# One core, attention with memory beside an MLP: two PSUM banks read crosswise, weight loads in streams of their own, and a new written-out order of all jobs

## The chip, the core and the metric

The kernel runs on one core of one Trainium2 chip. The metric is device time in microseconds (us) of one execution. Three runs of the kernel before gave 691.15, 692.08 and 692.50; the median is 692.08.

## The reference, cut to what matters

```python
x  = A_x                                  # 1 x 2048 x 512
xn = layernorm(x)
out = x + A(xn) + B(xn)

# A: 32 heads of 16, four segments of 512 positions
q, k, v = xn @ wq, xn @ wk, xn @ wv
for s in range(4):
    p     = softmax(q_s k_s^T * scale + causal mask)
    a_dot = p @ v_s
    a_mem = (phi(q_s) @ M) / (phi(q_s) @ z + 1e-6)      # the memory part; M = z = 0 for s = 0
    o_s   = g * a_mem + (1 - g) * a_dot                  # g = sigmoid(beta), one per head
    M, z  = M + phi(k_s)^T v_s, z + sum(phi(k_s))        # phi(t) = t + 1 for t > 0, else exp(t)
A = concat(o_s) @ wo

# B: MLP, 512 -> 1792 -> 512
B = gelu(layernorm(xn) @ w1 + b1) @ w2 + b2
```

All inputs and the output are fp32.

## The kernel before, in words

Products that need fp32 accuracy are made of three fp16 products (high x high, high x low, low x high), so weights and activations are split into a high and a low half first. The attention work is cut into 16 units: unit i is segment i // 4 and group i % 4 of eight heads. The MLP is cut into 16 pieces j: 256 positions and one half of the 1792 hidden columns.

The program is one long list of 1308 small jobs. `streams()` gives lists of jobs, each list in its own fixed order; the string `ORDER` names, letter by letter, from which list the next job is taken; `BANKS` says, digit by digit, which of the eight PSUM banks the next tile gets. Both were written ahead of time by a planner that is not part of the kernel. Each engine executes its own instructions in the order in which the jobs issue them, and waits at semaphores. A moved job thus moves on every engine and queue that it uses. The jobs that the texts below name:

- `("wl", m, k)` loads a part of a weight (SyncE's queue), `wm` sums its squares, `wf` makes a scale of the sum, `ws` splits a piece into halves. Parts are "qk", "QK", "RK" (the first, second, and last two groups of wq and wk), "v", "1a", "1b" (halves of w1), "2a", "2b", "o". `("par",)` loads beta and b1, `("par2",)` uses them. `X` loads and normalizes 256 positions, `Xt` transposes them, `ratio` makes a row of scales.
- `("T", i, 1)` and `("T", i, 0)` project keys and queries of unit i (twelve 512-column matmuls, L495), write the halves to DRAM (`kd`, `qd`) and read them back in another layout (`kst`, `qst`, L542).
- `M` finds row maxima of the scores: TensorE pairs on the upper and lower 64 rows (L636), VectorE reduces (L643). `R` sends the maxima through DRAM (`md`) into `qst`. `S` makes the scores again with the maximum taken off (L676), ScalarE takes exp (L681), GpSimd masks the diagonal (L690). `pv` and `PV` multiply with v (L705). `O` normalizes; its third part makes `oT` (L740, L741).
- `Z`, `Qd`, `Q`, `K`, `N`: the memory part. `Qd` is part 0 of `a_mem`: two products into two PSUM banks (L586), then ScalarE takes the denominator from one half of the partitions (L591) and VectorE the numerator from the other half (L592), for each bank. The tile `ame` has one buffer, and GpSimd still reads it for the unit before (L737).
- `D` is a column block of w1 (twelve 256-column matmuls), `G` gelu (another activation table is loaded for it, L778, and the first one again behind it, L896), `H` splits the result (GpSimd L785, ScalarE L786, GpSimd L787), `e` the product with w2 (six matmuls in pairs, L812), `out` the product with wo (L830), `A` loads the residual and adds b2, `warm` eight matmuls whose result nobody reads (L843).

Of the kernel before, what the change touches and what calls it, by code (L numbers as in the profile page):

```python
# [41 lines left out]
PARTS = ("qk", "QK", "v", "1a", "2a", "RK", "1b", "2b", "o")  # L42
LOADS = {"qk": 1, "QK": 1, "RK": 2, "v": 2, "1a": 2, "2a": 2, "1b": 3, "2b": 2, "o": 2}
# [12 lines left out]


def streams():
    keys, queries, nat, maxi, soft, vals_p, heads, memo, vals, norm, again, hid, act, mlp, outs, accs, wts = (
        [] for _ in range(17))  # L60
    for i in range(NU):
        s, g = divmod(i, NG)
        keys.append(("T", i, 1))
        queries.append(("T", i, 0))
        maxi += [("M", i, n) for n in range(12)] + [("R", i)]
        for h, ts in enumerate(((0, 2), (1, 3))):
            soft += [("S", i, t, n) for t in ts for n in range(3)]
            vals_p += [("pv", i, h, kb) for kb in range(3)] + [("PV", i, h)]
        heads += [("O", i, k) for k in range(3)]
        if s:  # L70
            memo += [("Z", i), ("Qd", i), ("Q", i)]
        if s < NSEG - 1:
            nat.append(("N", i))
            memo.append(("K", i))
        if g == 0:
            vals += [("V", s, b) for b in range(4)]
            outs += [("out", s, b) for b in range(4)]
    norm += [("X", 0, 0, 0), ("X", 0, 1, 0), ("X", 0, 0, 1), ("X", 0, 0, 2), ("X", 0, 1, 2)]
    for n in range(NSEG):
        for b in range(2):  # L80
            norm += [("X", n, b, k) for k in range(3)] * (n > 0) + [("Xt", n, b, k) for k in range(2)]
    again = [("ratio", n) for n in range(NSEG)]
    for j in range(NU):
        hf, fh = divmod(j, 2)
        hid += [("D", j, f) for f in range(FH)]
        act += [("G", j)] + [("H", j, c) for c in range(4)]
        if fh == 0:
            accs += [("A", 2 * hf + a, k) for a in range(2) for k in range(2)]
        mlp += [("e", j, n) for n in range(2 * FH)]
    for m in PARTS:  # L90
        if m != "RK":
            wts += [("wl", m, k) for k in range(LOADS[m])]
        if m == "qk":
            wts.append(("hold",))
        if m == "v":
            wts.append(("par",))
    split = [[("wm", m, k) for k in range(SQUARES[m])] + [("wf", m)] + [("ws", m, c) for c in range(len(SPLIT[m]))] +
             [("gate",)] * (m == "RK") for m in PARTS]
    zero = [("zero", 0), ("const",), ("zero", 1)]
    return [norm, again, wts, [("par2",)], zero, keys, queries, nat, maxi, soft, vals_p, heads, memo, vals, hid, act,  # L100
            mlp, outs, accs, [("warm", n) for n in range(14)], [("wl", "RK", k) for k in range(2)]] + split


ORDER = (
    "atacctcaetcttetcawvavcatwvcaxeacatxvdccwvxwfttyyyxbxyyuxgyyyzozoywouoxyccyzhoAzzAootAAppciiizAznpBiiABfBncAiBpi"
    "gzBszniipnzBiimchqqqiCBqBqiiioAoACBCCBCjjqiojqAjqjcioijoiCikskkBcmDskioBjiqiqCjjoijqCiqjsCqjDiftaoCCpgkkkpkjqCj"
    "oloojjljoloojiipkkkkiqihspqijqqipqijqiqjsjqqjaajfgpiiqkkkkmpliqqiooiqpDlqoDopohijjiojiijpolsjiqaqajqiqiqqiiqapk"
    "akmkktspaqijqiqjqiqajqbqajopijjgDfopkkkDkjjjlooooDlhjjjolqiqqiipkkkkjiqqijqqjjiqiqjjqiqiqiDkkkkmpliilfnplimpngr"
    "rmrjjponijqjqjinjipiskmkkmkaiijrijjoojiqsjqqjiqiiiqqkkkkihlqlfmlogojqjqjqqjjasoojmkkkkmqjiqjqjjaojjpipmooisikkk"
    "klpilhiofmgoooqiqpppqiqiqqqiiiqqpsosmoiqqiiqiqppsslooijqjojijojijoiaakkkkmpaijqjqjaqqqjiqqjiqjqiikmkkakbqiaqqah"  # L110
    "lolfqjjojqmjgjjoolmmkkkkmhjjoojjiitjiojiippkkkkliiilnfnimpligniinipmrrijjrsijqjqiqjiqjqiipkmkkksiqjqijqjqjiqjqi"
    "iqjqikmpkkkiprlqsphlfojmjgopjjlojpjoomokmkkkqiqisjojiqisjqiqijqqijqhiqqiiqjsqiiqppmkkkkilalofomqpgopaoooospmlaj"
    "qqqjqqjqjqiiqiqqqjqiqqipipooooiijooppoiaakkkkmajiqpisqqjiqjqjaiqaqhjqqqjqaaqmkkkkbjlfoljqjmjgojjqolmkkkkmmjjjoo"
    "jjioijoiiippkpkkkiinliifniiilnnimlgrpmjjrmjjjrrijikkpskkiqqijqiqijqqjiqjiqjqiqjiqiispqkpkskksqilqoplfojmjgjjjpo"
    "ooojolmkkkkiqjiqpsjiqiqijqjqiqijqjiqiqiqiiqqkksmkpikplolfjjqmjgjjjoooooklpkmkkjiiopjqiqijqjiqpjqiqijqiqqiqiiqik"
    "kpspkkqiplpoooopljjjqqqjqjjqooolkpskmkpkmqqqpqjpjqqqjqjqpqqjqjqqqkmkkkqlllqqqqqqqqqrrrr"
)

BANKS = (
    "050123614061756123401632157467410534702651305176254301741260523716405142730612547306651240651024615024612504612"
    "504650124650412650412650412650142650142650421607653420107642531076425031702531270531270531270132570132570132576"
    "135402761350427163054273106542736574326574326537425632754632574631072456310724563071245360712453620731620731067"
    "203617621073621073621073621037621037621037261702361475023671540263701524603175246031746013746013713460713471630"
    "471630463714067314056723410523674105236741052367410527410527410527410527410527140352671450326475103264751023674"
    "523674523647253647236547236475264735264107532410765324107265431067512043675120436751204736152047361520473615270"
    "346150312750317250317253107250371257013275027135027134650132754062751340621375460376054370567403056374065374065"
    "307645307645307642153076241076241076241076253410762534621075346210754316024310264310432610432610324610324612403"
    "246013752640163754207156437120564371205647312056473120564731206547321065473265104723607423460273460273642073642"  # L130
    "073642051736420157642031765420316750316705315631705630157630157630157306173504621357462017345620147536210436024"
    "136024316403216403216403216403216740536740536740536740536271406"
)


# [14 lines left out]
def infini_mixer_kernel(ctx: ExitStack, tc: tile.TileContext, x, wq, wk, wv, wo, beta, w1, b1, w2, b2, out):  # L150
# [15 lines left out]
    def dense():  # L166
        return dps.tile([P, 512], F32, name="ps" + next(bank), bufs=1)
# [385 lines left out]
    def log_recip(src, tmp):  # L553

        A.activation(tmp, src, AF.Ln)
        A.activation(tmp, tmp, AF.Exp, scale=-1.0)

    def newton(dst, src, tmp):

        V.tensor_tensor(src, src, tmp, op=OP.mult)  # L560
        V.scalar_tensor_tensor(dst, src, 2.0, tmp, op0=OP.subtract, op1=OP.mult)  # L561
# [18 lines left out]
    def a_mem(i, part):  # L580
        g = i % NG
        if part == 0:
            ps = dense(), dense()
            for b, p in enumerate(ps):
                r = slice(64 * b, 64 * b + 64)
                T.matmul(p, zrt[i][r], pqt[i, 0][r], start=True, stop=True)  # L586
            rd = rden[i] = sb.tile([P, 512], F32, name="rc")
            n = ame[i] = sb.tile([P, 512], F32, name="ame")
            for b, p in enumerate(ps):
                r, z = slice(64 * b, 64 * b + 64), slice(64 - 64 * b, 128 - 64 * b)  # L590
                A.activation(rd[r], p[z], AF.Copy, bias=1e-6, scale=qkcs[r, 0, g:g + 1])  # L591
                V.tensor_scalar(n[r], p[r], bg[r, g, 4:5], None, op0=OP.mult)  # L592
        else:
            rd = rden[i]
            t = sb.tile([P, 512], F32, name="rt")
            log_recip(rd, t)
            newton(rd, rd, t)
            G.tensor_tensor(ame[i], ame[i], rd, op=OP.mult)
# [275 lines left out]
    memo = {}  # L874

    def once(kind, n, make):
# [49 lines left out]
```

## Time and profile before

| | |
|---|---|
| profiled execution | 691.51 us, span 689.8 us |
| median of three runs | 692.08 us |
| TensorE busy | 681.8 us, 99% of the span |
| VectorE, ScalarE, GpSimd busy | 545.7, 502.9, 340.5 us |
| DMA traffic | 55.15 MB, 80 GB/s over the span |
| granted TensorE clock | 0.999 |

PE is TensorE, PEld its weight loads, DVE VectorE, ACT ScalarE, POOL GpSimd, SP SyncE, which only issues DMAs here. A matmul's end in this profile is modelled and matmuls overlap, so "busy" hides short waits; from the start of one matmul to the start of the next one sees more. In rows of a timeline and of the chain of waits the first number is the start and the second the length, in us.

### The profile page before, as it was taken

How to read it: one execution, taken by the hardware profiler on the slowest of the kernel's cores; microseconds unless marked ns; L12 is line 12 of the kernel's file. 1: busy time of each engine (PE TensorE's matmuls, PEld its weight loads, DVE VectorE, ACT ScalarE, POOL GpSimd, SP SyncE). 2: the span in 40 equal slices, each digit the busy share in tenths (PEclk: the TensorE clock that was granted, in tenths of full speed). 3: DMA queues.
4: the chain of work that ended last, by engine and by line, in shares of the span. 5: the costliest groups of instructions: out<-in, count | busy, mean ns of one | idle time of the engine just before them, and what ended most of it. 6: DMA issues, size and time to landing. Idle time of an engine off the chain costs nothing.

```text
span 689.8 us, 17163 instructions
## 1 busy us (share of the span) xinstructions
PE 681.8 (99%) x6465; PEld 399.8 (58%) x6465; DVE 545.7 (79%) x1740; ACT 502.9 (73%) x972; POOL 340.5 (49%) x526
## 2 busy tenths in 40 slices
PE   8999999999999999999999999999999999999997
PEld 7855655565654546566554557567564456656653
DVE  6999968897795887998797787888688696969442
ACT  4486897788786659856794796766795687878870
POOL 5355567456535334663435355454353545446752
PEclk9999999999999999999999999999999999999999
DMA  9856342421203322421213224231120415140101
GB/s 277 249 149 201 92 109 49 117 55 31 65 24 102 94 67 45 122 50 33 69 26 98 58 73 100 72 86 32 41 72 24 132 19 154 17 109 2 19 1 62
DMA packets 51792, 55.15 MB, mean 80 GB/s; under 512 B 4782, under 2 KB 40636, under 8 KB 51708
## 3 DMA queue, kind: packets, MB, share of 16 engines
q1 hardware_dynamic: 49404, 49.84, 24.9%
q0 software_dynamic: 2304, 4.20, 3.8%
q8 instruction: 51, 0.84, 0.5%
q14 instruction: 33, 0.27, 0.1%
HBM read 36.99 MB, written 17.04 MB: 78 GB/s over the span
## 4 chain that ended last, share of the span: by engine, by line
PE 85%; DVE 5%; ACT 5%; DMA 2%; POOL 1%; issue 1%; SPq 0%; POOLq 0%; DVEq 0%; ACTq 0%
PE ps L495 36%; PE ps L812 17%; PE ps L705 10%; PE ps L830 6%; PE ps L676 5%; PE ps L636 5%; DVE ps L643 3%; ACT pt L681 2%; PE ps L586 2%; PE ps L514 1%; PE ps L843 1%; PE ps L321 1%; DMA wks<-in_A_wk_dram 1%; DMA qd<-hl 1%; PE ps L617 1%
## 5 line engine op out<-in xcount | busy, mean ns | idle before, releaser
L643 DVE CUSTOM_DVE_ANT_0 ps<-ps,mask 128x512 f32<-128x512 f32 (+3 forms) x512 | 233.9, 523 | 14.1 <-PE ps L636 12.9
L681 ACT ACTIVATE pt<-ps,qkcs 128x512 f32<-128x512 f32 (+1 forms) x384 | 206.8, 624 | 37.3 <-PE ps L676 35.2
L812 PE MATMUL ps<-w2s,hT 64*128 64x512 f16 x1344 | 176.6, 375 | 0.1
L495 PE MATMUL ps<-xnT,w1s 128*128 128x256 f16 x1344 | 158.0, 273 | 0.0
L690 POOL TENSOR_SCALAR_AFFINE_SELECT pt<-pt 128x256 f32<-128x256 f32 x256 | 101.0, 421 | 98.2 <-ACT pt L681 97.2
L495 PEld LDWEIGHTS <-w1s 128*128 128x128 f16 x1344 | 127.2, 98 | 28.5 <-issue 11.6
L787 POOL TENSOR_TENSOR hT<-hh,hT 128x512 f16<-128x512 f32 x64 | 67.7, 1057 | 86.3 <-ACT hT L786 82.7
L812 PEld LDWEIGHTS <-hT 64*128 64x128 f16 x1344 | 76.3, 94 | 49.8 <-issue 5.9
L705 PE MATMUL ps<-pt,vt 128*32 128x512 f32 (+3 forms) x1024 | 77.1, 435 | 0.1
L771 DVE SCALAR_TENSOR_TENSOR hT<-ps,sc,sr 128x256 f32<-128x256 f32 x112 | 52.4, 478 | 26.9 <-PE ps L495 26.7
L643 DVE DVE_READ_ACCUMULATOR2_ANT mc<- 128x1 f32 x512 | 71.0, 139 | 0.0
L636 PE MATMUL ps<-kst,qst 48*128 48x256 f16 (+3 forms) x512 | 66.7, 297 | 1.1 <-DMA qst<-qd 0.3
L676 PE MATMUL ps<-qst,kst 50*128 50x512 f16 (+3 forms) x512 | 66.2, 297 | 0.0
L786 ACT ACTIVATE hT<-hh 128x512 f16<-128x512 f32 x64 | 36.6, 572 | 33.3 <-POOL hh L785 32.9
L705 PEld LDWEIGHTS ps<-pt,vt 128*32 128x32 f32 x1024 | 30.5, 109 | 43.0 <-issue 32.4
L785 POOL TENSOR_SCALAR hh<-hT,sc 128x512 f32<-128x512 f32 x64 | 42.2, 660 | 25.7 <-ACT hT L778 24.1
L735 POOL TENSOR_TENSOR nN<-nN,oT 128x512 f32<-128x512 f32 x16 | 20.3, 1269 | 61.1 <-DVE oT L561 61.1
L778 ACT ACTIVATE hT<-hT,b1t 128x256 f32<-128x256 f32 x112 | 46.5, 495 | 0.2
L495 PE MATMUL ps<-xnT,wqs 128*128 128x512 f16 x192 | 44.2, 380 | 0.0
L495 PE MATMUL ps<-xnT,wks 128*128 128x512 f16 x192 | 44.1, 379 | 0.0
L495 PE MATMUL ps<-wvs,xnT 128*128 128x512 f16 x192 | 44.0, 379 | 0.0
L830 PE MATMUL ps<-wos,oT 128*128 128x512 f16 x192 | 43.3, 379 | 0.6 <-POOL oT L741 0.6
(225 smaller groups left out, 883.1 us busy)
## 6 DMA issues: line engine op xcount, KB each, us to landing
kd<-hl SPq DMA_DIRECT2D x48, 128.0 KB
qd<-hl SPq DMA_DIRECT2D x48, 128.0 KB
kst<-kd SPq DMA_DIRECT2D x32, 192.0 KB
qst<-qd SPq DMA_DIRECT2D x32, 192.0 KB
acc<-in_A_x_dram SPq DMA_DIRECT2D x16, 256.0 KB
acc<-in_B_b_dram POOLq DMA_DIRECT2D x16, 256.0 KB, 4.2
out_dram<-acc SPq DMA_DIRECT2D x16, 256.0 KB
xt<-in_A_x_dram SPq DMA_DIRECT2D x14, 256.0 KB
```

The costliest lines, as they stand in the source:

```text
L495: T.matmul(p, wsl(ws, k, a), xsl(xs, k, b), start=s0 and i == 0, stop=s1 and i == 3 * n - 1)
L636: T.matmul(p[:, o:o + n], stk[i, 0][r, t, P * qb:P * qb + P], stk[i, 1][r, t, :n], start=True, stop=True)
L643: V.tensor_tensor_reduce(p[:, o:o + n], p[:, o:o + n], mask[:, 512 - n:], 1.0, -3e38, OP.add, OP.max, mc[:, 16 * b + 4 * t + qb:16 * b + 4 ...
L676: T.matmul(p[:, o:o + n], stk[i, 1][r, t, P * kb:P * kb + P], stk[i, 0][r, t, P * kb:], start=True, stop=True)
L681: A.activation(e[:, OFF[kbs[0]]:OFF[kbs[0]] + o], p[:, :o], AF.Exp, scale=qkcs[:, 1, i % NG:i % NG + 1])
L690: G.affine_select(v, v, pattern=[[0, 2], [1, P]], compare_op=OP.is_ge, fill=0.0, base=0, channel_multiplier=-1)
L705: T.matmul(p[32 * c:32 * c + 32, P * kb:], vt[s, kb][:, 4 * g + c, 16 * odd:16 * odd + 32], pt[i, 2 * c + odd][:, OFF[kb]:OFF[kb] + LEN[kb ...
L771: V.scalar_tensor_tensor(hz[:, fi, :], p[:, :256], col(F1 + fh), srow[hs][:, own], op0=OP.mult, op1=OP.mult)
L778: A.activation(z, z, AF.Gelu_apprx_tanh, bias=b1t[:, FH * (j % 2) + f:FH * (j % 2) + f + 1])
L787: G.tensor_tensor(hT[:, z, 1, :], t, hT[:, z, 0, :], op=OP.subtract)
L812: w = T.matmul(pes[j][a], hTs[fh][r, fi, u, P * a:P * a + P], w2s[r, fo, v, :], start=n == 0 and m == 0, stop=fi == FH - 1 and m == 2, ski ...
L830: T.matmul(p, o[:, u, P * b:P * b + P], wos[:, g, v, :], start=i == 0, stop=i == 3 * NG - 1)
```

## The change

Three edits. First, each weight part gets a stream of its own, so that its load can stand anywhere; before, all loads but those of "RK" were one stream, in which `hold` and `par` stood too. Second, `Qd` issues ScalarE's read of bank 0, VectorE's read of bank 1, ScalarE's of bank 1, VectorE's of bank 0; before, both engines read bank 0 and then bank 1. Third, `ORDER` and `BANKS` are written anew (1308 jobs and 1173 banks as before; a line of each is shown).

```diff
-    for m in PARTS:
-        if m != "RK":
-            wts += [("wl", m, k) for k in range(LOADS[m])]
-        if m == "qk":
-            wts.append(("hold",))
-        if m == "v":
-            wts.append(("par",))
+    wts = [[("wl", m, k) for k in range(LOADS[m])] for m in PARTS]
...
-    return [norm, again, wts, [("par2",)], zero, keys, queries, nat, maxi, soft, vals_p, heads, memo, vals, hid, act,
-            mlp, outs, accs, [("warm", n) for n in range(14)], [("wl", "RK", k) for k in range(2)]] + split
+    return [norm, again, [("hold",)], [("par",)], [("par2",)], zero, keys, queries, nat, maxi, soft, vals_p, heads, memo, vals, hid, act,
+            mlp, outs, accs, [("warm", n) for n in range(14)]] + wts + split
...
-    "atacctcaetcttetcawvavcatwvcaxeacatxvdccwvxwfttyyyxbxyyuxgyyyzozoywouoxyccyzhoAzzAootAAppciiizAznpBiiABfBncAiBpi"
+    "auauvfdcauufaExauuEaGxaGwEbyfaFFGyEaEGGuAzuFzegHHJHauFGJuGHiAHHhCHFIIBtHpHHppHIJppIpJpBjjqBJIIgjIqjtoKCIIoujqjK"
...
-    "050123614061756123401632157467410534702651305176254301741260523716405142730612547306651240651024615024612504612"
+    "012531714607252301476502431056712645213076407541623037541231607543273410265734012654012654061254065421065421056"
...
-            for b, p in enumerate(ps):
-                r, z = slice(64 * b, 64 * b + 64), slice(64 - 64 * b, 128 - 64 * b)
+            lo, hi = slice(0, 64), slice(64, 128)
+
+            def den(p, r, z):
                 A.activation(rd[r], p[z], AF.Copy, bias=1e-6, scale=qkcs[r, 0, g:g + 1])
+
+            def num(p, r):
                 V.tensor_scalar(n[r], p[r], bg[r, g, 4:5], None, op0=OP.mult)
+
+            den(ps[0], lo, hi)
+            num(ps[1], hi)
+            den(ps[1], hi, lo)
+            num(ps[0], lo)
```

Lines ahead of `a_mem` stand 6 lower in the new file and lines behind it 2 higher: L591 and L592 become L586 and L589, L542 becomes L536, L681 becomes L683.

Three places in the order of instructions follow; row names are those of the kernel, a number behind a name is the buffer.

SyncE, where unit 1's keys and queries go to DRAM and back, before:

```order
L534 DMA kd_94<-hl 8x16x512
L535 DMA kd_94<-hl 8x16x512
L536 DMA kd_94<-hl 8x16x512
L282 DMA w2s<-in_B_w_dram 128x5x512
L534 DMA qd_96<-hl 8x16x512
L535 DMA qd_96<-hl 8x16x512
L536 DMA qd_96<-hl 8x16x512
L542 DMA kst_92<-kd_94 48x4x512 x2
L542 DMA qst_90<-qd_96 48x4x512 x2
```

The same place now:

```order
L276 DMA w2s<-in_B_w_dram 128x5x512
L273 DMA w1s<-in_B_w_dram 128x5x128 x2
L793 DMA acc<-in_A_x_dram 128x512
L273 DMA w1s<-in_B_w_dram 128x5x128 x2
L266 DMA acc<-in_B_w_dram 128x4x128 x2
L528 DMA kd_94<-hl 8x16x512
L529 DMA kd_94<-hl 8x16x512
L530 DMA kd_94<-hl 8x16x512
L268 DMA oT<-in_B_w_dram 128x512 x2
L528 DMA qd_96<-hl 8x16x512
L529 DMA qd_96<-hl 8x16x512
L530 DMA qd_96<-hl 8x16x512
```

The 1280 KB load of w2 has moved from between the two sets of writes to ahead of both; two loads of 256 KB stand there now.

ScalarE around `Qd` of unit 11, with the semaphores that each row waits for, before:

```order
L681 ACTIVATE pt<-ps_7859,qkcs 128x256 [waits PE_49]
L681 ACTIVATE pt<-ps_7860,qkcs 128x256 [waits PE_49]
L591 ACTIVATE rc<-ps_7867,qkcs 64x512 [waits PE_49]
L591 ACTIVATE rc<-ps_7868,qkcs 64x512 [waits PE_49]
L681 ACTIVATE pt<-ps_7879,qkcs 128x512 [waits PE_49]
L681 ACTIVATE pt<-ps_7880,qkcs 128x512 [waits PE_49,Pool_49]
```

ScalarE there now:

```order
L683 ACTIVATE pt<-ps_7863,qkcs 128x512 [waits PE_49]
L683 ACTIVATE pt<-ps_7864,qkcs 128x512 [waits PE_49,Pool_49]
L586 ACTIVATE rc<-ps_7869,qkcs 64x512 [waits PE_49]
L586 ACTIVATE rc<-ps_7870,qkcs 64x512 [waits DVE_49]
L523 ACTIVATE hl<-ps_7879 128x512 [waits DMAHW3_49,DMAHW4_49,DMAHW2_49,PE_49]
L526 ACTIVATE phq<-ps_7879,qksc 128x512
```

The second read waits for VectorE now, and behind it stands the projection of the next unit in place of exps.

ScalarE near the end, from gelu of piece 14 to the first exps of unit 15, before:

```order
L778 ACTIVATE hT_115<-hT_115,b1t 128x256 x7
L786 ACTIVATE hT_115<-hh 128x2x256
L653 ACTIVATE mhl<-ps_9851 32x64
L653 ACTIVATE mhl<-ps_9852 32x64
L786 ACTIVATE hT_115<-hh 128x2x256
L896 ACT_TABLE_LOAD
L555 ACTIVATE nD<-oT 128x512
L556 ACTIVATE nD<-nD 128x512
L786 ACTIVATE hT_115<-hh 128x2x256
L786 ACTIVATE hT_115<-hh 128x256
```

The same place now:

```order
L780 ACTIVATE hT_115<-hT_115,b1t 128x256 x7
L788 ACTIVATE hT_115<-hh 128x2x256 x2
L655 ACTIVATE mhl<-ps_9849 32x64
L655 ACTIVATE mhl<-ps_9850 32x64
L788 ACTIVATE hT_115<-hh 128x2x256
L898 ACT_TABLE_LOAD
L549 ACTIVATE nD<-oT 128x512
L550 ACTIVATE nD<-nD 128x512
L788 ACTIVATE hT_115<-hh 128x256
```

Three copies of the split hidden layer stand ahead of the table load now, two did before.

More of the change, by code (lines that the diff above doesn't have):

```diff
@@ L58, in streams @@
 def streams():
-    keys, queries, nat, maxi, soft, vals_p, heads, memo, vals, norm, again, hid, act, mlp, outs, accs, wts = (
-        [] for _ in range(17))
+    keys, queries, nat, maxi, soft, vals_p, heads, memo, vals, norm, again, hid, act, mlp, outs, accs = (
+        [] for _ in range(16))
     for i in range(NU):
@@ L106 @@
[L106 to L115, printed above, removed]
@@ L116 @@
-    "kpspkkqiplpoooopljjjqqqjqjjqooolkpskmkpkmqqqpqjpjqqqjqjqpqqjqjqqqkmkkkqlllqqqqqqqqqrrrr"
+    "auauvfdcauufaExauuEaGxaGwEbyfaFFGyEaEGGuAzuFzegHHJHauFGJuGHiAHHhCHFIIBtHpHHppHIJppIpJpBjjqBJIIgjIqjtoKCIIoujqjK"
+    "jKKhKIJojqLqjoLjrjjrrrnJKLDrDjijKrjppKMLKJLtkJrkpkjrkjrjKJrkpkjpKjMLjllllpKkjtrjkpkjkrjLrLkLkgjnlLlLqltluhqppkL"
+    "krmppqmpkkkppkjrrjjmqlllljkrqrjkrkrjrkjrkrkarijgthpjrjqMrjjqrrnqlllljmappjjipqMkkmppkjkjpqkjrararjmkrjarjqjrtru"
+    "llanllktrjrarkjrkrbjraaMrkpnqpkjkhMqglalllkkmpqppkmikppkjrkrjjlllmlrjkrqjrkrjrkjrkjrkrrkjrjrMqjjllllMnjmmohmogs"
@@ new lines @@
+    "snkrkokkaopkjjskqjjllnllkqjjsnkktjppakjrrqkjrjrkrjjtlqlllirjmrmgpknhpkrkrkrkkptpllmlnlnkrjkrrkrkknpijkpjqjqjlll"
+    "lmtppmgpptqpnjqjhqrrrrjtrjjrqrjrqrjppjjrrjpjrjqmnrkrkppkkjpqjkpkjaajlqlllnrkjrakrkattrkrjnkrrirkrjjallllbarrjam"
+    "mpgpkrkrrkknkhpkmlnnlllkkpnpkipkjjkpukjjjqllllmojjmjgojmnjhojqjojqsqqsjkkskjrkrkrjrjrkjltlnllnkjrjrkjrknrkarkjr"
+    "rkjrjjqllttlqlsjmqripmgpkknhkkpprqkkpmpnllltlnjrkjrnrtiqkrjjrrjkpjrrjkrjrkjrrkjrjqjllllqmppmgjtnpqhppqppkrqrkra"
+    "rnkrrrkrjrjrtkrjrjrrjjmqppqppkjjajqpppjaalllqlnrjrqkarjrtkrirrakakjrrkrkrnraallllkrkmrmkgbknhpkkppllmnllnkkppnj"
@@ L117 @@
+    "kkpkjpjjklllqljqjojjqojmjqjjgmojnmhonskkksskkjsjkjllllnjkqrrjkrrjrkjrkjrkrktrjjrqjrttjlqlllrjmmrgprkknhppqpnkkk"
+    "npppmkjjlqllljjrkrjqrkjtrrkjrkjrkrrkjjrjrtqjllllrtjqmpmgrrkknqhpkkqppkkpmplnlltljjkqkjpkjrkjrkrjrkjrjrqjrjrqrjr"
+    "jrlllqljpqpmppqkmkrrrkkrkkrppptlmllnqqlnqrrrkqkrrkrrrrrkqkkrrrnrrllllrrrmrrrrrmmrrrssss"
 )
 BANKS = (
-    "050123614061756123401632157467410534702651305176254301741260523716405142730612547306651240651024615024612504612"
-    "504650124650412650412650412650142650142650421607653420107642531076425031702531270531270531270132570132570132576"
@@ L124 @@
[L124 to L132, printed above, removed]
+    "012531714607252301476502431056712645213076407541623037541231607543273410265734012654012654061254065421065421056"
@@ new lines @@
+    "421056421065421062514062514062514602514602514605021467324350167243507243502743052374035720437520437250431027456"
+    "310217405634217056340627315406257406274502674056270456247065247063752140623751406123754061237540612307361207361"
+    "207360127360127360127360172306176023637014015246732645017342635017345026170435261703461736041763064317430671604"
+    "173604173160471036471502367415023617450132467501234675034675034673504673540765431027654310276530412765310472652"
+    "047652047265047265407265405726405627405316247250134376520153476206145267301715604236175046234517063204517632307"
@@ new lines @@
+    "465123014723401721034721340712341072034172034102734610523712460572314560751476051047651047651045706145670145671"
+    "045623134705612035467501230451230453142503167436250174367204516324705163706513706513706513760513761075240137426"
+    "572301465672301425067531240675134206751304267513460274351620741634250702136457123604572134572413572413572413575"
+    "234123754615345021634765042137625047136125736125736151723651273635753126570431267504321673504216735246103752465"
+    "102546102645102645012641025641203561724601747216047246107246152"
```

## The prediction

> **What bounds the kernel now.** I read the page first, then TensorE's waits, then the chain of waits in order of time.
>
> ```profile
> span 689.8 us, 17163 instructions
> PE 681.8 (99%) x6465; PEld 399.8 (58%) x6465; DVE 545.7 (79%) x1740; ACT 502.9 (73%) x972; POOL 340.5 (49%) x526
> PE   8999999999999999999999999999999999999997
> PEclk9999999999999999999999999999999999999999
> ```
>
> TensorE is never idle for long in any slice and has its full clock; no other engine reaches 80%. The change neither adds nor drops an instruction (the counts of jobs are equal), so what it can alter is the time that TensorE spends between matmuls. For that I need the pace within a kind of work. Four rows of the chain give it (start, length, matmuls):
>
> ```profile
> 28.63 3.93 PE ps L495 x36
> 209.46 7.77 PE ps L830 x36
> 315.50 1.95 PE ps L812 x18
> 96.37 2.29 PE ps L705 x32
> ```
>
> That is 0.109 us for 256 columns, 0.216 for 512, 0.108 for each of two that run side by side on half the rows, and 0.072 for one of four side by side. The groups of instructions give the counts:
>
> ```profile
> L812 PE MATMUL ps<-w2s,hT 64*128 64x512 f16 x1344 | 176.6, 375 | 0.1
> L495 PE MATMUL ps<-xnT,w1s 128*128 128x256 f16 x1344 | 158.0, 273 | 0.0
> L705 PE MATMUL ps<-pt,vt 128*32 128x512 f32 (+3 forms) x1024 | 77.1, 435 | 0.1
> L636 PE MATMUL ps<-kst,qst 48*128 48x256 f16 (+3 forms) x512 | 66.7, 297 | 1.1 <-DMA qst<-qd 0.3 <-DVE mc L643 0.3
> L676 PE MATMUL ps<-qst,kst 50*128 50x512 f16 (+3 forms) x512 | 66.2, 297 | 0.0
> L830 PE MATMUL ps<-wos,oT 128*128 128x512 f16 x192 | 43.3, 379 | 0.6 <-POOL oT L741 0.6
> ```
>
> L812 makes 145.2, L495 on w1 146.5, L705 73.3, L636 and L676 together 69 (1024 in pairs, 320 columns in the mean, 0.135 a pair), and L830 with three groups of its size (q, k, v) 165.9. With some 42 for the small groups (an estimate by the same paces; the largest is 112 warm-ups at 0.109) this is 642.
>
> A change of the array's division costs extra:
>
> ```profile
> 636.20 5.41 PE L495 MATMUL ps<-xnT,w1s 128*128 128x256 f16 x48
> 641.54 0.55 PE L676 MATMUL ps<-qst,kst 50*128 50x512 f16 x4
> ```
>
> 48 at 0.109 end at 641.44; L676 begins at 641.54. So 0.10 for each change between full rows, half rows and quarter columns. Counted through the list of jobs there are 232 such changes, 22 us. 642 + 22 = 664, and TensorE works from 1.6 to 686.0, which is 684. Some 20 us are left, 2 of them the slow first warm-ups, and a few small items that my paces miss. **At most some 17 us, 2.5%, are waits**, and no order can save more. They are scattered; of those over 0.15 us at one place I count about 30, for VectorE's and ScalarE's reads of a bank, for DMAs, and at the end.
>
> The profiled execution took 691.5, 0.6 under the median of 692.08; I put the sum on the median.
>
> **The change part by part.**
>
> *Changes of division.* The new list has 227 of them: 5 x 0.10 = 0.5 us less, sure.
>
> *Start.* Same weights ahead of the first projection, another order of loads, and 512 KB of x for segment 1 moved into the first 25 us.
>
> ```profile
> 1.60 7.30 PE L843 MATMUL ps<-ones 128*128 128x256 f16 x48 [1.60 <-POOL ones L173]
> 9.44 0.62 PE L321 MATMUL ps<-wks 128*128 128x128 bf16 x8 [0.55 <-DMA wks<-in_A_wk_dram]
> 15.95 2.75 PE L495 MATMUL ps<-xnT,wks 128*128 128x512 f16 x12
> ```
>
> TensorE is filled with warm-ups up to the first weights at 9.44, and the first projection starts at 15.95. Now four warm-ups instead of six come first, then the first weights, and the v part, whose 1 MB is loaded ahead of "QK" now. There are eight warm-ups ahead of the first projection in both, and the row of scales (four transposes, 0.44) moves ahead of it, which costs nothing in total. I expect two or three gaps of about half a us while v lands, in place of the 0.55: 0.4 later, between -0.3 and +1.5. From there to 40 us TensorE has all its data by the old landing times, since the bytes ahead of w1 are the same; "RK" and the second x come earlier and w2's first half later by 512 KB, and the projection of unit 0's queries stands between as cover.
>
> *DRAM round trips.* Writes of `qd` have to land before their read is issued:
>
> ```profile
> 50.93 0.46 SPq L282 DMA_DIRECT2D w2s<-in_B_w_dram  x1
> 54.90 0.58 SPq L536 DMA_DIRECT2D qd<-hl  x1
> 60.34 1.41 SPq L542 DMA_DIRECT2D qst<-qd  x2
> 539.26 0.57 SPq L536 DMA_DIRECT2D qd<-hl  x1
> 542.29 0.79 SPq L542 DMA_DIRECT2D qst<-qd  x2
> 64.53 0.33 PEld L636 LDWEIGHTS <-qst 48*128 48x128 f16 x5 [0.68 <-DMA qst<-qd]
> ```
>
> 5.4 us for unit 1 with the 1280 KB load in flight, 3.0 for a late unit. That load is now ahead of both sets of writes, with 512 KB in its place, so I expect the 0.68 to go. Unit 2's x load goes from the same spot. Against it, the list leaves less TensorE work between projection and first `M` than before: counted with the paces above, 8.8 instead of 9.8 for unit 14 and 9.4 instead of 9.5 for unit 8. Net 0.3 less; bounds -1.3 (all these waits go) and +1.5.
>
> *Banks.* A bank of `M` is free when VectorE has reduced it:
>
> ```profile
> 48.88 0.50 PE L636 MATMUL ps<-kst,qst 48*128 48x256 f16 x4 [0.32 <-DVE mc L643]
> ```
>
> In the new list the tightest tenth of the banks behind a 512-column `M` is used again after 1.5 us of TensorE work or less, 1.2 before; behind `S` it is 1.5 in both. Waits like this one sum to some 6 us by the starts of matmuls; I take a tenth off, 0.6, between 0 and -3.
>
> *The crossing.* Two of the twelve `Qd` in the trace, ScalarE and VectorE:
>
> ```profile
> 249.53 1.39 ACT L591 ACTIVATE rc<-ps,qkcs 64x512 f32<-64x512 f32 x2
> 252.52 1.53 DVE L592 TENSOR_SCALAR ame<-ps,bg 64x512 f32<-64x512 f32 x2 [0.44 <-POOL nN L737]
> 499.35 1.39 ACT L591 ACTIVATE rc<-ps,qkcs 64x512 f32<-64x512 f32 x2
> 500.76 0.69 ACT L681 ACTIVATE pt<-ps,qkcs 128x512 f32<-128x512 f32 x1
> 501.67 1.53 DVE L592 TENSOR_SCALAR ame<-ps,bg 64x512 f32<-64x512 f32 x2 [2.73 <-POOL nN L737]
> ```
>
> Where VectorE is in time, the four reads take 1.4 us instead of 2.1. Where it is late, as here, ScalarE's second read, which did not wait, now does: in the first case until 252.52 + 0.77 = 253.29 instead of 250.23, 3.1 us, in the second 2.4, and behind it stand exps that free banks for TensorE. The same subtraction over all twelve gives 13 us of ScalarE held, against some 4 us of VectorE's waits saved. But in the new list the work between `O` of the unit before, whose GpSimd step VectorE waits for, and `Qd` is 3.4 instead of 1.1 us for unit 11 and 4.3 instead of 2.8 for unit 5, and behind unit 11's reads there are no exps. I take 0, between -1 and +5.4 (a rival, below).
>
> *End.* The chain from 636 on runs through ScalarE, and TensorE waits for it last of all:
>
> ```profile
> 628.45 0.27 PE L676 MATMUL ps<-qst,kst 50*128 50x256 f16 x1
> 663.77 1.89 ACT pt L681 x4
> 677.85 8.16 PE L830 MATMUL ps<-wos,oT 128*128 128x512 f16 x37 [0.63 <-POOL oT L741]
> ```
>
> From unit 14's last scores (628.45) to 686.0 are 57.5 us; the list has 54.2 of TensorE work in them, so 3.3 wait. In the new list 55.7 of work follow that point, 3.5 instead of 2.1 lie between unit 15's last scores and the product that needs their exps (663.77), and one job `e` more (eleven) stands between that product and `out`. Each late step of ScalarE thus gets 0.6 to 1.5 us more cover. Against it one more copy waits for GpSimd ahead of the table load. I take 1.0 off; bounds -2.6 and +1.0.
>
> Sum: -0.5 + 0.4 - 0.3 - 0.6 + 0 - 1.0 = -2.0, so **690.1 us**, a span of about 687.8. All that is certain in it is the 0.5.
>
> The clock at the start needs a word. 48 warm-ups at 0.109 would take 5.2 instead of 7.30, so about 19 ran at half the pace. Only 32 stand in one piece now, enough for those 19. The Trainium skill ("TensorE: Matmul & The Clock Gate", Part 1) says that the clock opens after a busy window of some 3.4 us that is not in step with the kernel; by that rule a pause could fall into the window and half the pace would last one window longer, 1.7 us by its figure, an estimate: 691.8. Nothing in the trace before shows such a pause.
>
> **Rivals.** *No change (691 to 693.4, say 692.2).* Waits move rather than go: the smallest distances of some banks shrink (behind a projection of w1 from 0.5 to 0.4, behind a 512-column `S` from 0.9 to 0.4), and the round trips give the rest back. That the terms above are all small, and each has a bound on the other side, speaks for it.
>
> *Slower by ScalarE's hold.* If the crossing holds ScalarE as computed, and 1.1 us of each hold is absorbed by the banks (half of the `S` banks are used again after 2.4 us, and exps of a pair take 1.25), the holds of 3.1, 2.7, 2.4, 2.0, 1.2 and so on leave 5.4 us on TensorE: 690.1 + 5.4 = 695.5. It decides from 3.4 us on. Against it stand the wider distances to `O`.
>
> *Much faster.* If the order really allows for all late steps, half of the 17 us goes: 684 to 687.
>
> **Chances.** My forecast (688.0 to 690.7) 0.40; much faster 0.10; no change 0.29 (the pause at the start, 691.8, has 0.03 of it); slower by the hold 0.15; slower because w1 or the v part lands 3.5 us or more late at the start 0.06. 0.2% (1.4 us) is about what a measurement here tells from nothing. Faster 0.50, same 0.29, slower 0.21. The range of 686.0 to 694.6 leaves out half of the fast case and the worst of the slow ones.
>
> **What would show it.** Right: the first projection near 16.5; no wait for `qst` near 65; ScalarE's waits for VectorE ahead of L586 a us each or less; the wait before `out` under 0.3. Wrong: ScalarE idle for 2 us and more at L586 with TensorE waiting for exps behind it; gaps over a us before 17 us; new waits for `qst` at units 8 and 14. It would be wrong altogether if TensorE's own pace changed.

## The result, and the profile after

| | median, us | runs | ratio to before, 95% interval |
|---|---|---|---|
| before, beside it | 691.96 | 7 | 1 |
| changed kernel | 695.3 (693.51 to 700.17) | 7 | 1.0058 (1.0039 to 1.0078) |
| changed kernel once more | 696.52 (694.78 to 697.13) | 5 | 1.0064 (1.0051 to 1.0076) |

The forecast was 690.1 with 686.0 to 694.6. The change made the kernel 0.6% slower, and its runs spread over 7 us where those of before spread over 2. The first profile is of the slowest run, 700.17 us; a second one, of a run of 696.18 us of the changed kernel once more, is used beside it. One run of the kernel before, beside the experiments, took 1391.8 us and is in no ratio. The page of the first profile:

```profile
span 698.5 us, 17165 instructions
PE 684.0 (98%) x6465; PEld 396.0 (57%) x6465; DVE 542.7 (78%) x1740; ACT 503.8 (72%) x972; POOL 340.4 (49%) x526
L638 PE MATMUL ps<-kst,qst 48*128 48x512 f16 (+3 forms) x512 | 66.6, 298 | 2.9 <-DMA qst<-qd 2.3
L678 PE MATMUL ps<-qst,kst 50*128 50x512 f16 (+3 forms) x512 | 66.6, 298 | 1.8 <-DMA qst<-md 0.9
```

Each engine executes as many instructions as before, and the groups keep their durations. The idle time ahead of L638 and L678 has grown, and it is now for DMAs. TensorE's waits, summed by what ended them, say where the loss lies (waiting line, releaser: total, times, longest):

```profile
PE ps L638 <- DMA qst<-qd: 2.3, 2, 1.7
PE ps L349 <- ACT w1s L308: 1.5, 3, 0.8
PE ps L678 <- DMA qst<-md: 0.9, 1, 0.9
PE ps L678 <- DVE hT L773: 0.8, 1, 0.8
PE ps L315 <- DMA w1s<-in_B_w_dram: 0.8, 1, 0.8
PE ps L814 <- DVE acc L820: 0.5, 1, 0.5
```

Since such idle times leave out what the modelled ends of matmuls cover, I also summed all waits from the starts of matmuls. Before and in the second profile of the changed kernel, in us: for the banks of `M` 3.5 and 0.8, of `S` 2.8 and 1.5, but for banks behind the `hT` steps 0.2 and 2.3; for `qd` read back 1.0 and 4.0, for `md` 0.8 and 2.1; for weights at the start 0.7 and 3.3, for sums of w1 0.1 and 0.9; ahead of `out` 0.9 and 0, for the last step of a piece (`acc`) 0.3 and 0.9. These are estimates by the prediction's paces, and those for banks depend on how small a delay still counts as a wait. What the order gained at the banks and ahead of `out` it lost to DMAs and at new places.

**The half clock.** TensorE around 54 us in the first profile (start, length; in brackets idle time and releaser), and the windows there (busy PE, PEld, DVE, ACT, POOL, granted clock, DMA share, GB/s):

```profile
54.52 0.38 PE L349 MATMUL ps<-am,ones 128*128 128x1 f32 x2 [0.78 <-ACT w1s L308]
55.28 0.38 PE L349 MATMUL ps<-am,ones 128*128 128x1 f32 x2 [0.37 <-ACT w1s L308]
56.03 0.38 PE L349 MATMUL ps<-am,ones 128*128 128x1 f32 x2 [0.37 <-ACT w1s L308]
56.50 4.44 PE L489 MATMUL ps<-wvs,xnT 128*128 128x512 f16 x12
61.30 2.76 PE L489 MATMUL ps<-wvs,xnT 128*128 128x512 f16 x12
```
```profile
54.00:56.00 2.00, 0.77 (x4) 0.59 (x4) 2.00 (x11) 1.94 (x7) 2.00 (x4) 1.00 0.58 196
56.00:58.00 2.00, 1.97 (x9) 1.11 (x10) 1.90 (x11) 0.93 (x3) 0.67 (x2) 0.71 0.07 12
58.00:60.00 2.00, 2.00 (x7) 0.63 (x6) 1.38 (x3) 0.00 (x0) 0.00 (x0) 0.50 0.60 189
60.00:62.00 2.00, 2.00 (x14) 0.81 (x13) 0.71 (x3) 1.03 (x3) 0.00 (x0) 0.94 0.76 197
```

From 53.7 to 56.5 us TensorE has nothing but matmuls of one column. The granted clock then falls to 0.50 for some 3.4 us (56.8 to 60.2, worked out from the clock of the last three windows), and twelve matmuls of 512 columns take 4.44 us instead of 2.76: the wait costs 1.7 us once more. It happens a second time near 300 us, behind the wait for unit 7's queries:

```profile
301.49 0.89 PE L638 MATMUL ps<-kst,qst 48*128 48x512 f16 x2 [1.70 <-DMA qst<-qd]
```
```profile
304.00:306.00 2.00, 2.00 (x12) 0.99 (x9) 1.03 (x5) 0.00 (x0) 0.00 (x0) 0.50 0.00 0
```

In the second profile the same wait was shorter and the clock stayed at 1.00. So a DMA that lands half a us later can cost two. That is one reason why the runs spread, not the only one: five of the seven have a mean clock of 1.000 and took 693.51 to 695.74 us, the other two 0.997 and 0.995 and took 697.48 and 700.17. The second profile:

```profile
299.04 0.39 PE L638 MATMUL ps<-kst,qst 48*128 48x512 f16 x1 [1.16 <-DMA qst<-qd]
```
```profile
302.00:304.00 2.00, 2.00 (x21) 1.22 (x21) 2.00 (x12) 0.00 (x0) 0.00 (x0) 1.00 0.00 0
```

### The profile page after: what moved, and what is told of

It reads as the page before. It is cut to its first block, busy times and chain, and to the rows that moved or that the text cites. A ratio compares the mean times of both kernels' runs of the same rounds, so it can differ in the third digit from the quotient of the medians.

```text
span 698.5 us, 17165 instructions
## 1 busy us (share of the span) xinstructions
PE 684.0 (98%) x6465; PEld 396.0 (57%) x6465; DVE 542.7 (78%) x1740; ACT 503.8 (72%) x972; POOL 340.4 (49%) x526
## 4 chain that ended last, share of the span: by engine, by line
PE 84%; DMA 7%; ACT 3%; DVE 2%; SPq 1%; issue 1%; POOL 0%; DVEq 0%; ACTq 0%
PE ps L489 33%; PE ps L814 20%; PE ps L707 9%; PE ps L832 6%; PE ps L678 5%; PE ps L638 5%; DMA qd<-hl 2%; DMA qst<-qd 2%; PE ps L580 1%; PE ps L508 1%; DMA w1s<-in_B_w_dram 1%; ACT pt L683 1%; DMA oT<-in_B_w_dram 1%; DMA wqs<-in_A_wq_dram 1%; PE ps L845 1%
## 5 line engine op out<-in xcount | busy, mean ns | idle before, releaser
L683 ACT ACTIVATE pt<-ps,qkcs 128x512 f32<-128x512 f32 (+1 forms) x384 | 208.3, 621 | 52.9 <-PE ps L678 49.3
L814 PEld LDWEIGHTS <-hT 64*128 64x128 f16 x1344 | 71.7, 94 | 54.9 <-issue 4.5
L638 PE MATMUL ps<-kst,qst 48*128 48x512 f16 (+3 forms) x512 | 66.6, 298 | 2.9 <-DMA qst<-qd 2.3
L678 PE MATMUL ps<-qst,kst 50*128 50x512 f16 (+3 forms) x512 | 66.6, 298 | 1.8 <-DMA qst<-md 0.9
L489 PE MATMUL ps<-wvs,xnT 128*128 128x512 f16 x192 | 45.7, 390 | 0.0
L678 PEld LDWEIGHTS <-kst 50*128 50x128 f16 x512 | 27.1, 94 | 31.2 <-issue 14.5
L638 PEld LDWEIGHTS <-qst 48*128 48x128 f16 x512 | 28.1, 95 | 28.4 <-issue 9.3
```

The source lines that it names most:

```text
L489: T.matmul(p, wsl(ws, k, a), xsl(xs, k, b), start=s0 and i == 0, stop=s1 and i == 3 * n - 1)
L638: T.matmul(p[:, o:o + n], stk[i, 0][r, t, P * qb:P * qb + P], stk[i, 1][r, t, :n], start=True, stop=True)
L678: T.matmul(p[:, o:o + n], stk[i, 1][r, t, P * kb:P * kb + P], stk[i, 0][r, t, P * kb:], start=True, stop=True)
L683: A.activation(e[:, OFF[kbs[0]]:OFF[kbs[0]] + o], p[:, :o], AF.Exp, scale=qkcs[:, 1, i % NG:i % NG + 1])
L814: w = T.matmul(pes[j][a], hTs[fh][r, fi, u, P * a:P * a + P], w2s[r, fo, v, :], start=n == 0 and m == 0, stop=fi == FH - 1 and m == 2, ski ...
```

## The experiments

Jobs are moved as in the change itself, by `ORDER` and `BANKS`; the diffs show the rows of the list of jobs. Every time stands beside runs of the kernel before on the same chip (medians 691.72 to 691.96).

**1. The changed kernel again, and three undoings: the reads, a load, and the crossing alone**

> The changed kernel itself once more, for a second profile and as the yardstick of the runs beside it. If the loss is in the order itself, the time is 695 again and the same waits come back: for the second half of w1 (2.3 us near 54 us), for the queries of units 7, 12 and 15 (2.4, 0.7, 1.0 us), two extra us ahead of the first query projection. If the profile caught chance delays of DMAs, most of these are other waits in this run; the half clock behind the wait at 54 us (1.7 us) should be absent where the wait stays under 2 us.

It gave 696.52 us, and the waits at 21, 54, 300, 515 and 646 us came back: they belong to the order.

The old sequence of reads in the new order:

```diff
             den(ps[0], lo, hi)
-            num(ps[1], hi)
+            num(ps[0], lo)
             den(ps[1], hi, lo)
-            num(ps[0], lo)
+            num(ps[1], hi)
```

> New order, the two banks read in the old sequence by both engines. Theory 'crossing costs': ScalarE loses its 10.4 us of waits for VectorE, the copies of the projections of units 11, 12 and 13 behind it come 1.3 to 2.7 us earlier, and their waits for the queries (0.1, 0.7, 0 us) go: 1.0 to 1.5 us faster than the changed kernel. Rival 'crossing is free': within 0.7 us of it. Rival 'crossing gains': the second bank is read later where VectorE is in time, 0.5 us or more slower.

696.98 us, ratio 1.0073 (1.0052 to 1.0094), against 1.0064: no difference within the intervals. Unit 12's wait went (0.7 us), unit 11's grew from 0.34 to 0.66, and in its profile the half clock fell behind unit 7. Inconclusive to 1 us; repeated below without the half clock.

```diff
 ("T", 0, 0)
-("wl", "2b", 0)          # 1280 KB of w2
 ...
 ("wl", "1b", 2)          # last of w1's second half
+("wl", "2b", 0)
```

> New order, with the 1280 KB load of w2 moved back behind the last load of the second half of w1. Theory 'load of w2 delays w1': 1280 KB at some 270 GB/s are 4.7 us, so the wait for w1 near 54 us (2.3 us) falls to 0.5 or less and the half clock behind it cannot come: 2 to 4 us faster than the changed kernel, 691.5 to 693. Rival 'the residual load of 256 KB and the busy queue do it': only 0.5 us faster. The load now stands just ahead of unit 1's writes, so its queries may land later: up to 0.7 us of wait there.

The wait near 54 us went, but the time was 695.78, 1.0058 (1.0044 to 1.0073). The profiled run lost the gain again near 300 us, by a wait of 1.8 us and the half clock behind it. One of the two long waits alone does not show in the median.

The crosswise reads as the only change to the kernel before (the diff of the change in `a_mem`):

> The kernel before with the crosswise reads as the only change. By the prediction's own sum 0 (between -1 and +5.4 us). Theory 'crossing costs': ScalarE waits some 13 us for VectorE over the twelve reads, exps stand behind several of them, and TensorE loses 1 to 3 us: 693 to 695. Rival 'crossing is free': within 0.7 us of before.

699.82 us, **1.0111 (1.0096 to 1.0126), 8 us slower**. The groups of the two readers, and ScalarE and TensorE at unit 11 (lines here: ScalarE L592, VectorE L595, exps L689, scores L684):

```profile
L592 ACT ACTIVATE rc<-ps,qkcs 64x512 f32<-64x512 f32 x24 | 16.4, 682 | 20.0 <-DVE ame L595 17.7 <-PE ps L586 1.9
L595 DVE TENSOR_SCALAR ame<-ps,bg 64x512 f32<-64x512 f32 x24 | 18.0, 750 | 10.3 <-POOL nN L745 7.1 <-PE ps L586 1.8 <-ACT rc L592 0.8
```
```profile
506.88 0.68 ACT L592 ACTIVATE rc<-ps,qkcs 64x512 f32<-64x512 f32 x1 [2.43 <-DVE ame L595]
507.58 1.26 ACT L689 ACTIVATE pt<-ps,qkcs 128x512 f32<-128x512 f32 x2
...
508.32 0.32 PE L684 MATMUL ps<-qst,kst 50*128 50x384 f16 x1 [0.76 <-ACT pt L689]
508.90 0.38 PE L684 MATMUL ps<-qst,kst 50*128 50x384 f16 x4 [0.26 <-ACT pt L689]
510.54 2.71 PE L495 MATMUL ps<-xnT,w1s 128*128 128x256 f16 x12 [0.51 <-ACT pt L689]
```

ScalarE waits 17.7 us for VectorE, which itself waits 7.1 for GpSimd, as before. At unit 11 ScalarE stands 2.43 us, the exps behind it come late, TensorE waits three times, and twelve matmuls then take 2.71 us where 1.47 is their time, at half the clock. The half clock is a small part of the 8 us: the run with a mean clock of 1.000 took 699.29. In the new order (profile after) ScalarE's wait at these reads is

```profile
L586 ACT ACTIVATE rc<-ps,qkcs 64x512 f32<-64x512 f32 x24 | 16.4, 683 | 11.2 <-DVE ame L589 10.4 <-PE ps L580 0.5
```

still 10.4 us, but little stands behind it that TensorE needs.

**2. Unit 7, the end, the start, and repairs together**

```diff
 ("T", 7, 0)
 ...
-("A", 6, 1)              # GpSimd's accumulating load of b2, 256 KB
 ...
 ("M", 7, 0)
+("A", 6, 1)
```

> New order, with one step moved: GpSimd's 256 KB accumulating load of b2 for the residual (L797), which stands beside unit 7's writes of the queries, behind unit 7's first M. Theory 'collision': the writes of qd land 5.3 us after their issue because this load and the read of kst share the queues; without it some 3.5, the wait of 1.4 to 1.9 us (and 0.5 us for the second half) near 300 us shrinks to 0.3 or less and the half clock of 3.3 us behind it never comes: 2 to 3.5 us faster than the changed kernel. Rival 'distance': the 9.8 us of TensorE work are too few whatever the load: 0.5 us or less faster.

The last write of `qd`, the read of it, and GpSimd's load, in the kernel before, in the changed kernel (second profile) and here:

```profile
285.99 0.57 SPq L536 DMA_DIRECT2D qd<-hl  x1
288.95 0.79 SPq L542 DMA_DIRECT2D qst<-qd  x2
294.61 0.89 POOL L795 DMA_DIRECT2D acc<-in_B_b_dram  x1 [1.31 <-DMA acc<-in_A_x_dram]
```
```profile
290.37 0.58 SPq L530 DMA_DIRECT2D qd<-hl  x1
290.51 0.88 POOL L797 DMA_DIRECT2D acc<-in_B_b_dram  x1
295.69 1.25 SPq L536 DMA_DIRECT2D qst<-qd  x2
```
```profile
288.79 0.58 SPq L530 DMA_DIRECT2D qd<-hl  x1
292.27 0.81 SPq L536 DMA_DIRECT2D qst<-qd  x2
294.16 0.88 POOL L797 DMA_DIRECT2D acc<-in_B_b_dram  x1
```

From write to read 5.3 us with the load beside it, 3.5 without, and TensorE no longer waits there. At this distance the load decides: the same 9.8 us of TensorE work (counted as in the prediction) stand in between in both. The distance has its part all the same, since the 15.2 us of the order before would have covered the longer way too. What the load and the writes share is not shown by these runs. The time, 695.06 or 1.0046 (1.0029 to 1.0062), is 1 us better in the median. Of its twelve runs the seven with a mean clock of 0.999 or 1.000 took 692.75 to 695.47, the five at 0.998 or less 696.19 to 697.89. That is probably the half clock at 54 us, since the load of w2 stands where it did; the profile, of the fastest of these runs, does not show it.

```diff
+("e", 13, 11), ("e", 13, 12), ("e", 13, 13)
 ("S", 15, 0, 0)
 ("O", 14, 1)
 ("S", 15, 0, 1)
-("e", 13, 11), ("e", 13, 12), ("e", 13, 13)
```

> New order, with the last three e jobs of piece 13 moved ahead of unit 15's first S, which waits for the maxima (0.9 to 1.1 us near 646 us); the next e job waits another 0.9 us for VectorE's last step of piece 13. Theory 'too little work between R and S': 2 us more work in between take both waits away, 1.5 to 2 us faster than the changed kernel. Rival 'the wait moves': ScalarE and VectorE are what is late, and the same time is lost at the next S or at the product with v: 0.5 us or less.

The wait moved and grew, 697.25 us, 1.0089 (1.0066 to 1.0112):

```profile
645.94 5.47 ACT L683 ACTIVATE pt<-ps,qkcs 128x512 f32<-128x512 f32 x10 [1.95 <-PE ps L678]
647.26 0.39 PE L678 MATMUL ps<-qst,kst 50*128 50x512 f16 x2 [1.02 <-ACT pt L683]
649.14 0.38 PE L678 MATMUL ps<-qst,kst 50*128 50x384 f16 x4 [0.41 <-ACT pt L683]
```
```profile
650.00:652.00 2.00, 2.00 (x11) 0.87 (x8) 0.00 (x0) 2.00 (x6) 2.00 (x4) 0.50 0.00 0
```

The `e` jobs had been the cover between scores, whose banks ScalarE empties one exp at a time; ahead of the scores they are missing there, and the clock fell. The rival held.

```diff
-("wl", "qk", 0), ("par",), ("wl", "v", 0), ("wl", "v", 1), ("wl", "QK", 0), ...
+("wl", "qk", 0), ("wl", "QK", 0), ("wl", "v", 0), ("wl", "v", 1), ("par",), ...
 ("T", 0, 1)
```

> New order, with the jobs up to the first key projection in the sequence of the kernel before (second q and k parts loaded ahead of v, small loads last, six warm-ups first); all later jobs as in the new order. Theory 'start': the new sequence costs 1.9 us (first projection at 17.4 instead of 15.95, 1.0 to 1.3 us of wait for w1 at 21), so this is 1.5 to 2 us faster than the changed kernel, with the first projection at 16 to 16.3. Rival 'the bytes set it': the wait for w1 grows by what the projection gains, 0.5 us or less.

A fault of this experiment, not of the start: the load of "RK", which the new order squares right behind w1, now stood behind unit 0's writes of the keys on SyncE's queue, and TensorE waited 6.0 us for it. 703.6 us, 1.0172 (1.0148 to 1.0195), says nothing on the start.

```profile
27.76 0.61 PE L315 MATMUL ps<-pt 128*128 128x128 bf16 x4 [6.01 <-DMA pt<-in_A_wk_dram]
```

> New order with all these moves together: the old start, the 1280 KB load of w2 behind the second half of w1, the b2 load behind unit 7's first M, two e jobs each ahead of the first M of units 10 and 11, three e jobs ahead of unit 15's first S. If the losses add up as read from the traces (1.9 start, 0.9 w1, 2 to 3.5 unit 7, 0.4 and 0.4 units 10 and 11, 1.9 end), it is 6 to 8 us faster than the changed kernel: 688 to 690.5, faster than the kernel before. If new waits take their place, it stays at 692 to 694.

704.13 us, 1.0175 (1.0158 to 1.0192): the same fault is in it, 5.5 us. Its later part shows that two `e` jobs ahead of the first `M` of units 10 and 11 took away the waits for the queries and gave waits for `M` banks instead (3.2 us of them in this run, 0.8 in the changed kernel).

**3. Heads exchanged, and the two loads together.** The list is cut behind unit 2's key projection (some 90 us); one kernel's jobs stand ahead of the cut and the other's remaining jobs behind it, with the banks renamed to fit.

```diff
 # new_head: jobs up to ("T", 2, 1) as in the changed kernel, the others (and the reads) as before
 # old_head: jobs up to ("T", 2, 1) as before, the others (and the reads) as in the changed kernel
 # old_head_add_later: the same, with ("A", 6, 1) moved behind ("M", 7, 0)
```

> The new order up to unit 2's key projection (some 90 us), from there the kernel before, old reads of the banks too. Theory 'the head costs': the late first projection and the wait for w1 at 21 us (1.5 to 2.5 us) and the wait for w1's second half near 54 us with its half clock (0.9 to 4 us) are all here: 2.5 to 5 us slower than before, with runs that spread over 4 us as those of the changed kernel do. Rival 'the rest costs': within 1.5 us of before.

694.3 us, 1.0032 (1.0021 to 1.0043): the head costs 2.4 us. In its profile the first projection starts at 17.52 and TensorE waits 1.2 us for w1 near 21.7, but it does not wait for the sums of w1 near 54 us, and all seven runs have a mean clock of 0.999 or 1.000. So here the start makes up most of the loss.

> The kernel before up to unit 2's key projection, from there the new order with its crosswise reads. Theory 'the head costs': no wait at 21 and 54 us; what stays is the collision at unit 7 (1.9 us and at times the half clock): 691.5 to 693.5. Rival 'the rest costs': 694 or more.

697.42 us, 1.0076 (1.0062 to 1.0089). The rival held: the rest costs more than the head. In its profile unit 7 waits 2.5 us, 1.83 of them in one piece, and the cut itself cost some 0.9 us near 96 us for VectorE. The two halves come to 2.4 and 5.5 us, together more than the whole change costs, so they can't be added up.

> As the run before, and the load of b2 moved behind unit 7's first M. If head and unit 7 are all that the new order loses, its gains at the banks and at the end are left: 689.5 to 691, faster than the kernel before. If the other late queries (units 10 to 12 and 15, 1.5 to 2 us) and the waits for VectorE and for the maxima near 580 and 645 us (3 us) weigh as much as those gains: 691 to 692.5.

694.36 us, 1.0033 (1.0020 to 1.0047): unit 7 alone is worth 3.1 us here. What stays is not a gain.

> New order with only two loads moved: the 1280 KB of w2 behind the second half of w1, and b2's load behind unit 7's first M. Both long waits at which TensorE drops to half its clock are then gone: no run under 0.998, 692 to 693.5 and a spread of 1 to 2 us instead of 3 to 6. Rival 'the half clock comes from something else': the same spread as the changed kernel.

693.16 us, **1.0016 (1.0006 to 1.0025)**. All eleven runs have a mean clock of 0.999 or 1.000. Two moved loads take back about 3 of the 4 us that the change lost.

**4. What was still open**

> New order with the two moved loads, and the jobs up to the first key projection in the sequence of the kernel before; the first part of RK is loaded where the new order loads it (its absence there made the earlier run with the old start wait 6 us at 22 us). Theory 'the start is the rest': first projection at 16.1 instead of 17.4 to 17.7, the waits for w1 near 21 us (0.4 to 1.7 us) smaller: 1 to 1.5 us faster than with the two loads alone, 691.6 to 692.2, level with the kernel before. Rival 'the later part is the rest': within 0.5 us of 693.2.

Two loads and the old start, with "RK" where the new order loads it: 692.2 us, 1.0013 (1.0004 to 1.0021). The first projection, ahead of which the changed kernel took 17.44 us, is at

```profile
16.00 2.75 PE L489 MATMUL ps<-xnT,wks 128*128 128x512 f16 x12
```

That is 1.4 us earlier, 0.44 of it for the row of scales, which follows later here. By the medians the start is worth 1.0 us, by the ratios 0.2, with intervals that overlap: its share is not settled.

> New order with the two moved loads and the old sequence of reads in the memory part. Theory 'crossing still costs': units 11 to 13 get their queries earlier, 0.5 to 1.2 us faster than with the crosswise reads. Rival 'the new order was made for the crossing': 0 to 1 us slower. In the old order the crossing cost 7.9 us.

692.84 us, 1.0012 (1.0004 to 1.0021), against 1.0016 with the crosswise reads: the same. In the new order the sequence of the reads is worth nothing that these intervals show.

> The kernel before, with one load moved: the 1280 KB of w2 ahead of w1's second half, where the new order has it. Theory 'this load makes the wait at 54 us': w1's second half lands some 4.7 us later, its sums end at 54 instead of 50, and TensorE waits 2 to 2.5 us at the sums near 52 us, with the half clock (1.7 us) in some runs; unit 1's queries wait 0.7 us less: 1.3 to 3.5 us slower than before. Rival 'the x load between the halves of w1 makes it': within 0.7 us of before.

691.73 us, 1.0001 (0.9992 to 1.0011). My theory was too simple: the load alone does no harm. It makes w1's second half late, and there was room for that. ScalarE's first sum of w1's second half, before, and then the first and the last one here:

```profile
44.16 1.47 ACT L314 ACTIVATE w1s<-w1s 128x1536 bf16<-128x1536 f32 x1
```
```profile
45.84 1.48 ACT L308 ACTIVATE w1s<-w1s 128x1536 bf16<-128x1536 f32 x1 [1.58 <-DMA w1s<-in_B_w_dram]
50.65 0.64 ACT L308 ACTIVATE w1s<-acc 128x512 bf16<-128x512 f32 x1
```

The first sum starts at 45.84 instead of 44.16 and the last one ends 1.6 us later, which the cover took up; and unit 1's wait for its queries is gone, as forecast. In the changed kernel that first sum starts at 50.24. Three moves meet there: 512 KB of x for segment 1 and 256 KB of the residual are ahead of it as well as the load of w2, and other steps of ScalarE stand between the sums. This is read from the order, and the other two moves were not tried alone. That such a head need not make TensorE wait shows in `new_head`, where the same loads stood ahead, the first sum started at 49.01 and no wait followed. The changed kernel, first profile:

```profile
50.24 1.48 ACT L308 ACTIVATE w1s<-w1s 128x1536 bf16<-128x1536 f32 x1 [2.79 <-DMA w1s<-in_B_w_dram]
53.34 1.04 ACT L308 ACTIVATE w1s<-w1s 128x1024 bf16<-128x1024 f32 x1
```

No version here beats the kernel before.

## Why the prediction was wrong

*DRAM round trips* (forecast -0.3, bounds -1.3 and +1.5) is the step that failed most. The waits for `qd` grew by 3.0 us, those for `md` by 1.3, and the half clock of 1.7 us comes on top in some runs. What it said of unit 1 came true: 3.1 us from write to read there (second profile) instead of 5.4, and no wait. But I compared the work between projection and `M` with a chain of fixed length and spoke of units 8 and 14. The chain is not fixed: at unit 7 the work fell from 15.2 to 9.8 us, still nearly enough for a chain of 10, but GpSimd's load of b2 had moved beside the writes and made it 11.7. I followed SyncE's queue and not GpSimd's. The removal of that load from the place shows the cause: 9.6 us, and no wait.

*Start* (+0.4, bounds -0.3 and +1.5) failed too. The first projection came at 17.4 instead of 16.5, and w1's first half is waited for. The changed kernel, first profile:

```profile
17.44 2.76 PE L489 MATMUL ps<-xnT,wks 128*128 128x512 f16 x12
21.16 1.61 PE L315 MATMUL ps<-w1s 128*128 128x128 bf16 x25 [0.79 <-DMA w1s<-in_B_w_dram]
```

I wrote that TensorE has all its data from then to 40 us "since the bytes ahead of w1 are the same". The bytes ahead of w1's first half were the same, and TensorE waited for it near 21 us nevertheless, 0.8 us here and 1.1 in the second profile. For the second half some 2 MB were newly ahead, and I had costed the 1280 KB load by what its absence relieves, not by what its new place delays. That wait took 0.9 us in the quieter profile, 2.3 and a half clock in the other.

*The slow clock* stood in the prediction as a rival for the start alone. The pause at the start did not come: the clock opened at 5.6 us there and at 5.5 before. The slow clock came later, behind long waits or several short ones, and made a term of 2 us into one of nearly 4. The Trainium skill ("TensorE: Matmul & The Clock Gate", Part 1) gives an idle window of some 3.4 us for the fall. Here less was enough: the clock fell about 1 us after the end of a wait of 1.70, and behind three short waits of 1.02, 0.41 and 0.20. The last section counts how much idle time it took.

*Banks* (-0.6): right in kind. The waits for banks of `M` and `S` fell by 4.0 us, but those for banks behind late `hT` steps gave 2.1 back: -1.8 or so, within its bounds. The size is uncertain: if only delays over 0.12 us are counted, the same starts give some -0.5.

*End* (-1.0): -0.1. From unit 14's last scores to the last matmul 57.0 us before and 58.4 now, with 54.2 and 55.7 of work in them. The wait ahead of `out` fell from 0.9 to nothing, as forecast; in its place came 1.1 for `md` and 0.9 for VectorE at unit 15.

*Crossing* (0, rival +5.4): the mechanism was right, the rival's sum too small. In the old order the two holds that I worked out, 3.1 and 2.4 us, came as 3.10 and 2.43. But ScalarE stood 17.7 us in all, not 13, and the price was 8 us rather than 5.4 (the five holds listed, less 1.1 each, already leave 5.9), most of it at the full clock. In the new order the price is 0, and not for the reason given first: the wider distance to `O` did not shorten the hold at unit 11, where ScalarE stood 2.7 us for VectorE. What stood behind it decided. The other reason, that there are no exps behind unit 11's reads, left something out: behind them stand the copies of the projection, and unit 12's queries came 0.7 us late for it; the gain of undoing that was lost again elsewhere.

*Changes of division* (-0.5): the traces have five fewer, as forecast, but half a us can't be told apart in these runs. The 22 us for all of them is a slip without weight here: 232 at 0.10 are 23.

## What to carry to other kernels

Where a reordering moves transfers, follow every queue past every wait: for each moved load, list what it now stands ahead of, on GpSimd's queue too, and add up the moves that meet at one place; each of them alone may be harmless. On a saturated TensorE price a wait by its length and, where waits close together come to some 1.4 us, by the half clock that may follow, which cost 1.7 us here. A cross-engine wait such as the crossing has no price of its own: the same edit cost 8 us in one order and nothing in another, by what stood behind it.

## What the runs showed of the hardware

The half clock goes by steps of time and not by the length of one wait. In the first profile the clock opens at 5.63 us and falls at 56.83 and 302.59, which is 15 and 87 times 3.413 us later, and each half clock lasts 3.41 us. In the other 16 profiles, too, every change that follows the opening, the fall behind the last matmul included, comes a whole multiple of 3.413 us after it. Counted in these steps, TensorE's idle time (by the modelled ends) was 1.34 to 1.81 us in the step before each fall, and 3.41 where "RK" came late. In the steps behind which the clock stayed at 1.00 it was at most 1.41. So even a longer wait can pass. This one of `old_head` fell into two steps, 1.36 us in the first and 0.47 in the second:

```profile
299.27 0.89 PE L638 MATMUL ps<-kst,qst 48*128 48x512 f16 x2 [1.83 <-DMA qst<-qd]
```
```profile
302.00:304.00 2.00, 2.00 (x20) 1.23 (x20) 2.00 (x12) 0.00 (x0) 0.00 (x0) 1.00 0.00 0
```

In `before_crosswise` three waits of 0.76, 0.26 and 0.51 us in one step brought the clock down. Some 1.4 us of idle time in one step is thus the limit that these 17 profiles suggest, an estimate. Where the steps lie differs from run to run, so the same order can lose the clock in one run and keep it in the next.

VectorE's scaled copy of an fp32 tile within SBUF (L538) stops for GpSimd. It takes 0.48 us alone; where a GpSimd product of 1.16 us had begun 0.03 us ahead, it took 1.40, which is the rest of that product and 0.28. Of the 24 such copies in the second profile, eight that began while a GpSimd instruction ran took 0.55 to 1.40 us, and each of them ended 0.28 us after that instruction. The longest:

```profile
580.60 1.16 POOL L789 TENSOR_TENSOR hT<-hh,hT 128x512 f16<-128x512 f32 x1 [2.20 <-ACT hT L788]
580.63 1.40 DVE L538 TENSOR_SCALAR phq<-phq,qksc 128x512 f32<-128x512 f32 x1
583.60 0.70 PE L678 MATMUL ps<-qst,kst 50*128 50x256 f16 x7 [0.84 <-DVE hT L773]
```

The Trainium skill ("SBUF — State Buffer", "SBUF: two separate sides") describes such a lock between the two engines, and the rows agree. The `hT` steps behind the copy start late, and TensorE waits for them up to 583.6 us. That this copy is the whole of that wait was read from the trace, not tried.
